# Numerators of batches 1 to 3 as float32 products on quarters of the array

## The chip, the core and the metric

The kernel runs on one core of a Trainium2 chip. A core has five engines that run side by side: TensorE (PE in the profile, with PEld for its loads of the stationary operand), VectorE (DVE), ScalarE (ACT), GpSimd (POOL), and SyncE (SP), which issues the DMAs. The metric is the time of one execution on the device, in microseconds (us); lower is better.

## The reference

Four batches go through a linear attention and then a gated layer whose gate mixes over the sequence. Cut to what matters:

```python
# batch 4, heads 4, seq 1088, head_dim 32, r = 8: 64 features per head
phi(x) = outer(S1 @ x, S2 @ x)                    # 64 products per position
kv = sum over seq of phi(k) * v                   # 64 x 32 per head
z = sum over seq of phi(k)
x = (phi(q) @ kv) / (phi(q) @ z + 1e-6)           # numerator / denominator
h = relu(x @ w_in); u, v = halves of h            # 512 + 512 columns
v_n = (v - mean(v)) / sqrt(var(v) + 1e-6)
out = (u * (w_spatial @ v_n + b_spatial)) @ w_out
```

The product with `w_spatial` (1088 x 1088 by 1088 x 512 for each batch) is most of the work.

## The kernel before

**Two kinds of product.** Large products are made of three float32r products each (`mm3`, lines 461 to 463): an operand x is split into a rounded high half (float32r) and a low half (x minus the high half), and high by high, high by low and low by high are added up in PSUM. A float32 product does without the split. The kernel has float32 products where operands are small: the projections of keys (L624), the sums over keys (L674) and the projections of queries (L797).

**Stages.** Batch 0's attention comes first and is written differently. The attention of batch b+1 (`attention`) is mixed into the large product of batch b (`main`, lines 1042 to 1053); batch 3's large product is another scheme (`main_fast`, lines 1314 to 1327). In `attention` a batch's 1088 positions are taken as three groups g of 384, 384 and 320 columns (`TW`). For each group and each pair of heads pr:

- DMAs bring the two factors `fa` and `fb` of the query features into slots of tag `pl`, and GpSimd multiplies them in place (L817). This is f, 128 features (two heads of 64) by n columns.
- ScalarE rounds f to its high half `fh` (L544) and GpSimd makes the low half `fl` (L474). Both lie in slots of tag `r`.
- TensorE takes `mm3` of f with `kvh`/`kvl`, the two halves of a 128 x 128 matrix for each pair with numerators and denominators of both heads and zeros between the heads. The result `nd` fills one PSUM bank of tag `sd` (there are two such banks).
- ScalarE takes the denominators out (L876, with 1e-6 added) and the numerators (L877), 64 partitions at a time, so that they lie alike.

Then VectorE takes the reciprocal (L878) and multiplies (L879), ScalarE and VectorE split the result into `xh` and `xl` (L544, L471), and three `mm3` with `w_in` make the h product (`hidden_v`, out to `sd` banks, ScalarE's L898).

The 128 x 128 matrices come from `kv`, the sums over keys: one ScalarE copy out of PSUM (L716), four VectorE products with a mask (L857), one cast and one subtraction (L544, L471).

**Order.** `ORDER` is a table of operation numbers, found beforehand by a planner. It sets the order of the instructions on every engine, the DMA queue's too; an engine does its instructions in this order and waits where an operand isn't ready. A prime mark behind a number chooses the other engine for an operation that has one.

Of the kernel before, what the change touches and what calls it, by code (L numbers as in the profile page):

```python
# [9 lines left out]
F32 = mybir.dt.float32  # L10
# [32 lines left out]
BIAS = [(0, 8, 53), (8, 4, 83), (12, 4, 83)]  # L43

# [11 lines left out]
    "pl": 6, "c": 3, "r": 4, "abT": 2, "kt": 3, "v": 3, "ka": 2, "kp": 3, "kvh": 1, "kvl": 1,  # L56
# [1515 lines left out]
```

## Time and profile before

| | |
|---|---|
| Time, median of 3 runs | 318.69 us (318.4 to 319.26) |
| Profiled execution | 318.51 us, of which the span shown is 316.7 us |
| PE busy | 311.3 us, 2717 products |
| DVE busy | 237.7 us |
| ACT busy | 171.8 us |
| POOL busy | 48.4 us |

The span runs from the first to the last instruction of the program; some 1.8 us of the execution lie around it. "Busy" is the time in which at least one instruction of the engine was under way. A PE product's record reaches from its start to the modelled end of its results, and the next one starts earlier than that: what a product takes from the engine is the distance from its start to the next start.

### The profile page before, as it was taken

How to read it: one execution, taken by the hardware profiler on the slowest of the kernel's cores; microseconds unless marked ns; L12 is line 12 of the kernel's file. 1: busy time of each engine (PE TensorE's matmuls, PEld its weight loads, DVE VectorE, ACT ScalarE, POOL GpSimd, SP SyncE). 2: the span in 40 equal slices, each digit the busy share in tenths (PEclk: the TensorE clock that was granted, in tenths of full speed). 3: DMA queues.
4: the chain of work that ended last, by engine and by line, in shares of the span. 5: the costliest groups of instructions: out<-in, count | busy, mean ns of one | idle time of the engine just before them, and what ended most of it. 6: DMA issues, size and time to landing. Idle time of an engine off the chain costs nothing.

```text
span 316.7 us, 7095 instructions
## 1 busy us (share of the span) xinstructions
PE 311.3 (98%) x2717; PEld 298.3 (94%) x2717; DVE 237.7 (75%) x551; ACT 171.8 (54%) x423; POOL 48.4 (15%) x63
## 2 busy tenths in 40 slices
PE   7999999999999999999999999999999999999996
PEld 6887999999999999999889999999999999999995
DVE  5999997365787956558896789879887987863445
ACT  2499956445774354465637557563254468442432
POOL 2000100764600001642003352100000000000000
PEclk9999999999999999999999999999999999999999
DMA  6942256646213036510113433422122333210001
GB/s 207 330 146 68 72 168 190 209 124 184 59 52 96 14 106 190 170 41 0 50 35 108 132 120 84 123 59 78 54 73 54 91 99 108 79 38 2 0 2 70
DMA packets 26019, 30.77 MB, mean 97 GB/s; under 512 B 3330, under 2 KB 25730, under 8 KB 25986
## 3 DMA queue, kind: packets, MB, share of 16 engines
q1 hardware_dynamic: 25986, 30.33, 32.1%
q8 instruction: 21, 0.34, 0.5%
q14 instruction: 12, 0.10, 0.1%
HBM read 27.25 MB, written 3.06 MB: 96 GB/s over the span
## 4 chain that ended last, share of the span: by engine, by line
PE 97%; DVE 1%; issue 0%; ACT 0%
PE sp L1042 16%; PE sp L1044 14%; PE sp L1051 14%; PE sd L461 4%; PE sd L462 4%; PE sd L463 4%; PE pu L461 3%; PE sd L1314 3%; PE sd L1316 3%; PE sd L1315 3%; PE pu L462 2%; PE pu L463 2%; PE po L461 2%; PE sp L1314 2%; PE sp L1316 2%; PE sp L1315 2%
## 5 line engine op out<-in xcount | busy, mean ns | idle before, releaser
L1042 PE MATMUL sp<-wT,vh 128*128 128x332 f32 (+1 forms) x306 | 98.8, 323 | 0.0
L1044 PE MATMUL sp<-wT,vl 128*128 128x332 f32 (+1 forms) x272 | 87.6, 322 | 0.0
L1051 PE MATMUL sp<-wT,vh 128*128 128x332 f32 (+1 forms) x272 | 85.9, 321 | 0.0
L1042 PEld LDWEIGHTS sp<-wT,vh 128*128 128x128 f32 x306 | 57.5, 188 | 1.8 <-issue 0.8
L1044 PEld LDWEIGHTS sp<-wT,vl 128*128 128x128 f32 x272 | 51.1, 188 | 0.6
L1051 PEld LDWEIGHTS sp<-wT,vh 128*128 128x128 f32 x272 | 51.0, 188 | 0.1
L900 DVE BATCH_NORM_STATS2 small<-vt 128x6 f32<-128x512 f32 x36 | 24.2, 683 | 7.1 <-ACT vt L898 7.1
L1078 DVE TENSOR_TENSOR u<-sp,u 128x332 f32<-128x332 f32 (+1 forms) x32 | 16.7, 523 | 17.0 <-PE sp L1053 9.1
L898 ACT ACTIVATE vt<-sd 128x512 f32<-128x512 f32 x36 | 21.5, 601 | 11.4 <-PE sd L463 10.6
L878 DVE RECIPROCAL area<-area 128x384 f32<-128x384 f32 (+1 forms) x9 | 21.7, 2415 | 7.5 <-ACT area L876 7.5
L817 POOL TENSOR_TENSOR area<-area 128x384 f32<-128x384 f32 (+1 forms) x18 | 17.3, 970 | 56.2 <-DVE vh L967 26.5
L544 ACT CAST g<-u 128x332 fp32r<-128x332 f32 (+1 forms) x32 | 15.5, 487 | 18.0 <-DVE u L1078 9.4
L474 POOL TENSOR_TENSOR area<-area,area 128x384 fp32r<-128x384 f32 (+1 forms) x18 | 18.0, 1006 | 19.8 <-ACT area L544 9.7
L1034 ACT ACTIVATE u<-pu 128x332 f32<-128x332 f32 (+1 forms) x32 | 14.9, 467 | 10.8 <-PE pu L463 9.5
L471 DVE TENSOR_TENSOR g<-u,g 128x332 fp32r<-128x332 f32 (+1 forms) x32 | 17.2, 536 | 2.5 <-ACT g L544 1.4
L596 ACT CAST wT<-area 128x332 fp32r<-128x332 f32 (+1 forms) x27 | 12.4, 495 | 9.4 <-DMA area<-in_wT 9.2
L631 DVE TENSOR_TENSOR area<-ka,sd 128x768 f32<-128x768 f32 x15 | 13.7, 947 | 4.3 <-ACT ka L629 4.2
L461 PE MATMUL pu<-x,wih 128*128 128x332 f32 (+3 forms) x52 | 16.6, 320 | 0.0
L462 PE MATMUL pu<-x,wih 128*128 128x332 f32 (+3 forms) x52 | 16.3, 314 | 0.0
L463 PE MATMUL pu<-x,wil 128*128 128x332 f32 (+3 forms) x52 | 16.3, 314 | 0.0
L920 DVE TENSOR_SCALAR vt<-vt,small 128x512 f32<-128x512 f32 x31 | 15.9, 537 | 0.0
L958 ACT CAST vh<-vt 128x384 fp32r<-128x384 f32 x24 | 12.1, 516 | 6.8 <-DVE vt L920 6.8
(239 smaller groups left out, 762.5 us busy)
## 6 DMA issues: line engine op xcount, KB each, us to landing
w<-in_wT SPq DMA_DIRECT2D x48, 138.0 KB
area<-in_wT SPq DMA_DIRECT2D x18, 166.0 KB
area<-in_vA SPq DMA_DIRECT2D x12, 198.0 KB
area<-in_kT SPq DMA_DIRECT2D x12, 192.0 KB
area<-abd SPq DMA_DIRECT2D x24, 96.0 KB
area<-abd SPq DMA_DIRECT2D x12, 192.0 KB
area<-in_wT SPq DMA_DIRECT2D x9, 212.0 KB
area<-in_qT SPq DMA_DIRECT2D x7, 192.0 KB
```

The lines of the kernel that those rows point to most:

```text
L461: nc.tensor.matmul(o, ah, bh, start=start, stop=False)
L462: nc.tensor.matmul(o, ah, bl, start=False, stop=False)
L463: nc.tensor.matmul(o, al, bh, start=False, stop=stop)
L471: return lambda: nc.vector.tensor_tensor(out=o(), in0=a(), in1=bb(), op=ALU.subtract)
L474: return lambda: nc.gpsimd.tensor_tensor(out=o(), in0=a(), in1=bb(), op=ALU.subtract)
L817: op("POOL", c_pool(n), lambda fa=fa, fb=fb: nc.gpsimd.tensor_tensor(out=fa[:, :n], in0=fa[:, :n], in1=fb[:, :n], op=ALU.mult), r=[fb], w= ...
L878: op("DVE", 135 + 6.3 * n, lambda x32=x32, n=n: nc.vector.reciprocal(out=x32[:, :n], in_=x32[:, :n]), w=[x32])
L898: op("ACT", c_act(512, True) + 16, lambda pv=pv, t=t: nc.scalar.activation(vt[:, t], pv.ap, AF.Relu), r=[pv], w=[(vt, toks(t))])
L900: op("DVE", 690, lambda stats=stats, t=t: nc.vector.bn_stats(out=stats.ap, in_=vt[:, t]), r=[(vt, toks(t))], w=[stats])
L1042: nc.tensor.matmul(sp[:, :cw], vh[:, kt], wTh[:, kt, cs], start=(kt == 0), stop=False)
L1044: nc.tensor.matmul(sp[:, :cw], vl[:, kt], wTh[:, kt, cs], start=False, stop=False)
L1051: nc.tensor.matmul(sp[:, :cw], vh[:, kt], wTl[:, kt, cs], start=False, stop=False)
```

## The change

1. The split of f, `fh`, `fl`, `kvh`, `kvl` and the mask products are gone. In their place a group has four float32 products of 64 x 64 by n columns, one on each quarter of the array: rows (features) of head a, columns of pair pr. Those of a = 0 write one `sd` bank, those of a = 1 the other, and the pair chooses the upper or lower 64 partitions.
2. `kd`, the 64 x 64 blocks, is written by two ScalarE copies out of PSUM in place of L716, L857 and the split.
3. Numerators and denominators now lie interleaved by 32 partitions, so they are taken out in six pieces (two of 128 partitions that write more than is wanted, and four of 32 that put it right) in place of four. Each piece has ScalarE and, as the other choice, VectorE.
4. The room of tag `r` goes to four more slots of tag `pl` (10 in place of 6) and to `kd`.
5. `ORDER` is new from the 449th entry on, sought with a charge for each change between float32 and float32r on TensorE.

```diff
-    "pl": 6, "c": 3, "r": 4, "abT": 2, "kt": 3, "v": 3, "ka": 2, "kp": 3, "kvh": 1, "kvl": 1,
+    "pl": 10, "c": 3, "abT": 2, "kt": 3, "v": 3, "ka": 2, "kp": 3, "kd": 2,
...
-419 441 564 399 384 442 443 444 560 561 415 385 400 445 565 421 422 423 424 425 426 427 428 429 267 554 258 579 259 268 562 420 260 530 531 532 580 111 282 269 563 546 279 541
+419 441 564 399 384 442 443 444 560 561 415 385 400 445 565 421 422 423 424 425 426 427 428 429 267 554 258 259 268 562 420 260 530 531 532 111 282 269 563 546 279 541 433 466
...
-        kvs = tl("ka", f"kvs{b}", [P, 68])
-        op("ACT", c_act(68, True), lambda: nc.scalar.copy(out=kvs.ap, in_=kv[:, :68]), r=[kv], w=[kvs])
-        return kvs
+        kd = tl("kd", f"kd{b}", [P, 2, 2, D])
+        def half(den):
+            o = kv[:, :68].rearrange("p (r c) -> p r c", r=2)
+            return nc.scalar.copy(out=kd[:, :, den], in_=o[:, :, D:D + 1].broadcast_to([P, 2, D]) if den else o[:, :, :D])
+
+        for den in range(2):
+            op("ACT", c_act(64, True), lambda den=den: half(den), r=[kv], w=[(kd, den)])
+        return kd
...
+            fs = [query_fs[b, g, pr] for pr in range(2)]
+            nds = [bank("sd", f"nd{b}{g}{a}") for a in range(2)]
+
+            def sums(fs=fs, nds=nds, n=n):
+                for pr in range(2):
+                    for a in range(2):
+                        rows = slice(64 * a, 64 * a + 64)
+                        nc.tensor.matmul(nds[a][64 * pr:64 * pr + 64, :n], kd[rows, pr].rearrange("p q d -> p (q d)"), fs[pr][rows, :n], start=True, stop=True)
+
+            op("PE", n * 4 / 2.35 + 220, f4=True, fn=sums, r=[kd, *fs], w=nds)
+
+            def take(out, a, den, q, at, key, n=n, nds=nds):
+                rows, src = slice(32 * q, 32 * q + at), nds[a]
+                i = slice(32 * (q ^ 1), 32 * (q ^ 1) + 32) if at == 32 else rows
+
+                def act():
+                    if den:
+                        return nc.scalar.activation(out[rows, :n], src[i, :n], AF.Copy, bias=ATT_EPS)
+                    return nc.scalar.copy(out=out[rows, :n], in_=src[i, :n])
+
+                def dve():
+                    if den:
+                        return nc.vector.tensor_scalar_add(out[rows, :n], src[i, :n], ATT_EPS)
+                    return nc.vector.tensor_copy(out=out[rows, :n], in_=src[i, :n])
+
+                op("ACT", c_act(n, True), act, r=[src], w=[(out, key)], alts=[("DVE", c_dve(n), dve)])
+
+            take(xn, 0, 0, 0, P, None)
+            take(x32, 1, 1, 0, P, None)
             for pr in range(2):
-                f = query_fs[b, g, pr]
-                fh, fl = tl("r", f"fh{b}{g}{pr}", [P, 384], F32R), tl("r", f"fl{b}{g}{pr}", [P, 384], F32R)
-                split(lambda fh=fh, n=n: fh[:, :n], lambda fl=fl, n=n: fl[:, :n], lambda f=f, n=n: f[:, :n], n, [f], [fh], [fl], pool=True)
-                nd = bank("sd", f"nd{b}{g}{pr}")
-                op("PE", c_mm(n, 3), cls=(n, 3), fn=lambda nd=nd, fh=fh, fl=fl, pr=pr, n=n: mm3(nd[:, :n], kvh[:, pr], kvl[:, pr], fh[:, :n], fl[:, :n]), r=[kvh, kvl, fh, fl], w=[nd])
...
+                take(xn, 1, 0, 2 * pr + 1, 32, pr)
+                take(x32, 0, 1, 2 * pr, 32, pr)
```

On TensorE, batch 1's first group stands at the same place of the order. Before (`pu0` is a gate product, `sd` the numerators' banks, `sp1` the large product's sum, `area2` the room of `fh`, `fl`, `kvh` and `kvl`):

```order
L463 MATMUL pu0_187<-x_77,wil0_72 128x332
L461 MATMUL sd0_94<-area2_80 128x384
L462 MATMUL sd0_94<-area2_80 128x384
L463 MATMUL sd0_94<-area2_80 128x384
L461 MATMUL sd1_119<-area2_80 128x384
L462 MATMUL sd1_119<-area2_80 128x384
L463 MATMUL sd1_119<-area2_80 128x384
L1042 MATMUL sp1_276<-wT_74,vh_67 128x332
```

And in the changed kernel (line numbers are two to sixteen higher there; `area2` now holds `kd` and slots of `pl`):

```order
L465 MATMUL pu0_187<-x_77,wil0_72 128x332
L869 MATMUL sd0_94<-area2_80 64x384
L869 MATMUL sd1_119<-area2_80 64x384
L869 MATMUL sd0_94<-area2_80 64x384
L869 MATMUL sd1_119<-area2_80 64x384
L1058 MATMUL sp1_276<-wT_74,vh_67 128x332
```

Six float32r products became four float32 products in a row, which alternate between the two banks, with float32r products before and behind them.

On ScalarE, what stands between batch 1's sums over keys and the first h product before (`ka0<-sd1` takes the sums out, `area2<-area0` rounds the matrices, `wT<-area1` rounds a piece of `w_spatial`, `area0<-po2` takes a result of batch 0 out, `x<-area1` rounds the attention's result, `vt<-sd0` is the h product's):

```order
L716 COPY ka0_63<-sd1_119 128x68
L544 CAST area2_80<-area0_78 128x256
L596 CAST wT_74<-area1_79 128x332
L1015 COPY area0_78<-po2_262 128x424
L876 ACTIVATE area1_79<-sd0_94 64x384
L876 ACTIVATE area1_79<-sd1_119 64x384
L1034 ACTIVATE u1_243<-pu0_187 128x332
L877 COPY area1_79<-sd0_94 64x384
L544 CAST area2_80<-area1_79 128x384
L877 COPY area1_79<-sd1_119 64x384
L544 CAST g_698<-u0_239 128x332
L544 CAST x_77<-area1_79 128x384
```

And in the changed kernel:

```order
L720 COPY area2_80<-sd1_119 128x2x32
L598 CAST wT_74<-area1_79 128x332
L1031 COPY area0_78<-po2_262 128x424
L879 ACTIVATE area1_79<-sd1_119 128x384
L879 ACTIVATE area1_79<-sd0_94 32x384 x2
L1050 ACTIVATE u1_243<-pu0_187 128x332
L880 COPY area1_79<-sd0_94 128x384
L880 COPY area1_79<-sd1_119 32x384 x2
L546 CAST g_698<-u0_239 128x332
L546 CAST x_77<-area1_79 128x384
```

Three pieces of denominators stand ahead of the reciprocal where two stood, and three pieces of numerators behind it where two stood; the round of f is gone.

On ScalarE in batch 2, from the first group's h products to the second group's numerators before (`vt<-sd` takes an h product out, the bank's number is behind `sd`):

```order
L898 ACTIVATE vt_82<-sd1_119 128x512
L898 ACTIVATE vt_82<-sd0_94 128x512
L544 CAST g_698<-u1_243 128x424
L898 ACTIVATE vt_82<-sd1_119 128x512
L544 CAST area2_80<-area1_79 128x320
L876 ACTIVATE area1_79<-sd0_94 64x384
L1034 ACTIVATE u2_250<-pu0_187 128x332
L876 ACTIVATE area1_79<-sd1_119 64x384
```

And in the changed kernel:

```order
L914 ACTIVATE vt_82<-sd1_119 128x512
L914 ACTIVATE vt_82<-sd0_94 128x512
L546 CAST g_698<-u2_250 128x424
L879 ACTIVATE area1_79<-sd0_94 128x384
L880 COPY area1_79<-sd1_119 128x384
L1050 ACTIVATE u0_239<-pu0_187 128x332
L880 COPY area1_79<-sd0_94 32x384 x2
L914 ACTIVATE vt_82<-sd0_94 128x512
```

The third h product of the first group moved behind the second group's numerators, and it takes bank `sd0` when the last of these pieces is out. On TensorE twelve products of the large one and three of the output, all of 424 columns, stand between those numerators and that h product.

## Rows read from the trace of the kernel before

**Rows 1.** The page: busy time of PE, and its granted clock in 40 slices.

```profile
PE 311.3 (98%) x2717; PEld 298.3 (94%) x2717; DVE 237.7 (75%) x551; ACT 171.8 (54%) x423; POOL 48.4 (15%) x63
...
PEclk9999999999999999999999999999999999999999
```

**Rows 2.** The page: chain that ended last, by engine.

```profile
PE 97%; DVE 1%; issue 0%; ACT 0%
```

**Rows 3.** Busy time in two stretches: us, each engine (instructions), clock, DMA share.

```profile
30.00:70.88 40.88, 40.88 (x435) 39.68 (x435) 30.04 (x68) 25.76 (x60) 12.14 (x15) 1.00 0.52 152
213.00:300.00 87.00, 87.00 (x623) 86.66 (x622) 65.99 (x164) 39.36 (x107) 0.00 (x0) 1.00 0.23 63
```

**Rows 4.** Timeline of PE, numerators of 384 columns, then 320: start, length.

```profile
70.88 0.34 PE L461 MATMUL sd<-area 128*128 128x384 f32 x1
...
71.77 0.34 PE L463 MATMUL sd<-area 128*128 128x384 f32 x1
71.94 0.32 PE L1042 MATMUL sp<-wT,vh 128*128 128x332 f32 x1
...
200.89 0.31 PE L461 MATMUL sd<-area 128*128 128x320 f32 x1
...
201.61 0.31 PE L463 MATMUL sd<-area 128*128 128x320 f32 x1
201.76 0.32 PE L1042 MATMUL sp<-wT,vh 128*128 128x332 f32 x1
```

**Rows 5.** Groups of PE by line and form: count, busy us, mean ns.

```profile
L461 PE MATMUL sd<-area 128*128 128x384 f32 x12 | 4.0, 337 | 0.0
...
L461 PE MATMUL sd<-area 128*128 128x320 f32 x6 | 1.9, 316 | 0.0
```

**Rows 6.** Timeline of PE, two late starts among the numerators.

```profile
92.27 0.36 PE L461 MATMUL sd<-area 128*128 128x320 f32 x1
92.47 0.31 PE L462 MATMUL sd<-area 128*128 128x320 f32 x1
...
130.31 0.44 PE L462 MATMUL sd<-area 128*128 128x384 f32 x1
130.59 0.34 PE L463 MATMUL sd<-area 128*128 128x384 f32 x1
```

**Rows 7.** Timeline of PE, from float32r to float32 (L674) and back.

```profile
66.69 0.31 PE L1044 MATMUL sp<-wT,vl 128*128 128x332 f32 x1
66.83 0.31 PE L1051 MATMUL sp<-wT,vh 128*128 128x332 f32 x1
67.07 1.73 PE L674 MATMUL sd<-area 128*32 128x33 f32 x144
68.73 0.47 PE L461 MATMUL po<-x,woh 128*128 128x424 f32 x1
69.04 0.35 PE L462 MATMUL po<-x,woh 128*128 128x424 f32 x1
69.23 0.35 PE L463 MATMUL po<-x,wol 128*128 128x424 f32 x1
```

**Rows 8.** Timeline of PE, float32 products of 192 columns on halves and on quarters of the columns.

```profile
22.16 0.87 PE L797 MATMUL po<-u,sk 128*64 128x192 f32 x8
22.96 0.50 PE L461 MATMUL sd<-wi,x 128*128 128x512 f32 x1
...
106.35 0.51 PE L797 MATMUL sd<-area,sk 128*32 128x192 f32 x8
106.79 0.46 PE L1042 MATMUL sp<-wT,vh 128*128 128x424 f32 x1
```

**Rows 9.** Timelines of ACT, DVE and PE: batch 1's first group, denominators to h product.

```profile
72.84 1.00 ACT L876 ACTIVATE area<-sd 64x384 f32<-64x384 f32 x2
...
73.87 2.55 DVE L878 RECIPROCAL area<-area 128x384 f32<-128x384 f32 x1 [2.84 <-ACT area L876]
...
77.67 0.56 DVE L471 TENSOR_TENSOR x<-area,x 128x384 fp32r<-128x384 f32 x1 [0.58 <-ACT x L544]
...
78.42 0.40 PE L461 MATMUL sd<-wi,x 128*128 128x512 f32 x1
```

More of the change, by code (lines that the diff above doesn't have):

```diff
@@ L43 @@
 BIAS = [(0, 8, 53), (8, 4, 83), (12, 4, 83)]
+PL_MIDDLE, EXTRA = 6, 2048
 TW = (384, 384, 320)
@@ L98 @@
 270 555 437 356 230 534 409 261 410 411 412 369 370 535 556 271 397 398 438 439 440 277 262 402 403 413 25 26 414 278 266 275 559 558 533 529 542 434 435 263 371 386 272 536
[40 rows of a table removed]
[10 rows of a table added]
+955 832 956 966 968 967 758 971 969 785 786 787 788 703 945 972' 970' 973 740 974 789 780 790 756 946 781 975 976 791 998 1000' 754 1002 1004 999 1003 1001 1005 1006 1007 755
[6 rows of a table added]
+1311 1054 1314 1139 1315 1318 1055 1319 1196 1044 879 1331 1409 1035 1316 1419 1317 1140 878 1333 1335 1332 1420 1337' 880 1410 1336 1338 1411 1421 1334 1339 1144 1340 1045
+1046 1047 1048 1049 1050 1423 1290 1293 1291 1341 1292 1296 1059 1060 1061 1062 1063 1064 882 1069 881 863 1065 1051 1052 1053 1193 1433 1342 1343 1094 1095 1096 1097 1098 1422
+1432 1434 1312 1313 1363 1365' 1090 1435 1066 1143 1367 1369 1424 1364 1436 1320 1370 1089 1427 864 1437 1428 1425 1426 1366 883 1070 1368 1371 1372 1091 884 1071 1072 1073
[19 rows of a table added]
 """
@@ L378, in tile_kernel @@
     early = {"kt": 384, "v": 396, "kp": 768}
-    middle = {"c": 384, "abT": 192, "pl": 424}
-    extra = {"r": 384, "kvh": 256, "kvl": 256}
-    parts = (early, middle, extra)
-    sizes = [sum(n * Order.bufs(t) for t, n in part.items()) for part in parts]
-    areas = [const.tile([P, n], F32R if j == 2 else F32, name=f"area{j}", tag=f"area{j}", bufs=1) for j, n in enumerate(sizes)]
-    spans, again = [], {2: areas[2]}
+    middle = {"c": (384, 0, 3), "abT": (192, 0, 2), "pl": (424, 0, PL_MIDDLE)}
+    extra = {"pl": (424, PL_MIDDLE, Order.bufs("pl")), "kd": (128, 0, 2)}
+    parts = ({t: (n, 0, Order.bufs(t)) for t, n in early.items()}, middle, extra)
+    sizes = [max(sum(n * (e - a) for n, a, e in part.values()), EXTRA * (j == 2)) for j, part in enumerate(parts)]
+    areas = [const.tile([P, n], F32, name=f"area{j}", tag=f"area{j}", bufs=1) for j, n in enumerate(sizes)]
+    spans, again = [], {}
     for j, (area, part) in enumerate(zip(areas, parts)):
         end = 0
-        for tag, n in part.items():
-            m = Order.bufs(tag)
-            homes[tag] = area[:, end:end + m * n].rearrange("p (n c) -> p n c", n=m)
-            homes |= {(tag, i): homes[tag][:, i] for i in range(m)}
+        for tag, (n, a, e) in part.items():
+            m = e - a
+            home = area[:, end:end + m * n].rearrange("p (n c) -> p n c", n=m)
+            if m == Order.bufs(tag):
+                homes[tag] = home
+            homes |= {(tag, a + i): home[:, i] for i in range(m)}
             spans += [(j, end + i * n, end + i * n + n, tag) for i in range(m)]
@@ L849, in attention @@
         k.part = "k", f"k{b}"
-        kv = keys(b, qts)
-        kd = tl("kp", f"kd{b}", [P, 4, 2, D])
-        for pr in range(2):
-            for den in range(2):
-                def part(pr=pr, den=den):
-                    v = kv[:, 34 * pr:34 * pr + D + 1].unsqueeze(1)
-                    src = (v[:, :, D:] if den else v[:, :, :D]).broadcast_to([P, 2, D])
-                    return nc.vector.tensor_tensor(out=kd[:, 1 + pr if den else 3 * pr], in0=src, in1=mask[:, 2:4].unsqueeze(2).broadcast_to([P, 2, D]), op=ALU.mult)
-                op("DVE", 215, part, r=[kv, mask], w=[(kd, (pr, den))], sh=True)
-        kvh, kvl = tl("kvh", f"kvh{b}", [P, 2, P], F32R), tl("kvl", f"kvl{b}", [P, 2, P], F32R)
-        split(
-            lambda: kvh.ap.rearrange("p r c -> p (r c)"), lambda: kvl.ap.rearrange("p r c -> p (r c)"), lambda: kd.ap.rearrange("p q a d -> p (q a d)"),
-            256, [kd], [kvh], [kvl],
-        )
+        kd = keys(b, qts)
         for g in range(3):
@@ L868, in attention @@
             x32, xn = tl("c", f"x32{b}{g}", [P, 384]), tl("c", f"xn{b}{g}", [P, 384])
-            for pr in range(2):
-                f = query_fs[b, g, pr]
-                fh, fl = tl("r", f"fh{b}{g}{pr}", [P, 384], F32R), tl("r", f"fl{b}{g}{pr}", [P, 384], F32R)
-                split(lambda fh=fh, n=n: fh[:, :n], lambda fl=fl, n=n: fl[:, :n], lambda f=f, n=n: f[:, :n], n, [f], [fh], [fl], pool=True)
-                nd = bank("sd", f"nd{b}{g}{pr}")
-                op("PE", c_mm(n, 3), cls=(n, 3), fn=lambda nd=nd, fh=fh, fl=fl, pr=pr, n=n: mm3(nd[:, :n], kvh[:, pr], kvl[:, pr], fh[:, :n], fl[:, :n]), r=[kvh, kvl, fh, fl], w=[nd])
-                rows, den = slice(64 * pr, 64 * pr + 64), slice(64 - 64 * pr, 128 - 64 * pr)
-                op("ACT", c_act(n, True), lambda nd=nd, x32=x32, rows=rows, den=den, n=n: nc.scalar.activation(x32[rows, :n], nd[den, :n], AF.Copy, bias=ATT_EPS), r=[nd], w=[(x32, pr)])
-                op("ACT", c_act(n, True), lambda nd=nd, xn=xn, rows=rows, n=n: nc.scalar.copy(out=xn[rows, :n], in_=nd[rows, :n]), r=[nd], w=[(xn, pr)])
+            fs = [query_fs[b, g, pr] for pr in range(2)]
@@ L1082, in gate @@
             else:
-                tag = "r" if last(d) else "g"
-                gh, gl = tl(tag, f"gh{b}{d}{c}", [P, cw], F32R), tl(tag, f"gl{b}{d}{c}", [P, cw], F32R)
+                gh, gl = tl("g", f"gh{b}{d}{c}", [P, cw], F32R), tl("g", f"gl{b}{d}{c}", [P, cw], F32R)
                 parts = [(lambda: gh.ap, gh), (lambda: gl.ap, gl)]
@@ L1141, in weights_fast @@
     def weights_fast():
-        whole = {tag: Whole(k, tag, f"s_{tag}", [P, n], F32 if part is not extra else F32R) for part in parts for tag, n in part.items()}
+        whole = {tag: Whole(k, tag, f"s_{tag}", [P, n]) for part in parts for tag, (n, _, _) in part.items()}
         whole["g"] = Whole(k, "g", "s_g", [P, G_PITCH], F32R)
```

73 rows, old and new, of the table ORDER are left out of this document.

## The prediction

> **What bounds the kernel now.** I read the page first: PE is busy for 311.3 of 316.7 us, at the full granted clock in all 40 slices [rows 1]. The chain that ended last is 97% PE and 1% DVE [rows 2], so the end is set by TensorE. Busy shares are averages, so I then took stretches: from 30 us to the end of batch 1's sums, and from 213 to 300 us, PE is busy for every microsecond, while DVE has 30.04 of 40.88 and 65.99 of 87.00 [rows 3]. The reader is to see that there is hardly any idle time on PE to win. What can shorten this kernel is less work on PE, and what can lengthen it is more work on PE or a wait put in front of it. Work taken from ScalarE, VectorE and GpSimd counts only through such a wait.
>
> A busy PE is not yet a PE at its peak, since records overlap. So I go by distances between starts: a float32r product of 384 columns takes (71.94 - 70.88) / 6 = 0.177 us, one of 320 columns (201.76 - 200.89) / 6 = 0.145 us [rows 4]. Products of 332 columns follow each other at 0.14 to 0.15 us and those of 424 at 0.19 us [rows 7].
>
> **What is removed from PE.** The two groups of rows are those of the first line of `mm3`, with 12 and 6 products [rows 5]; the other two lines have as many, so 36 products of 384 columns and 18 of 320 go: 36 x 0.177 + 18 x 0.145 = 6.37 + 2.61 = 8.98 us. Two of them carried a wait inside the numerators: a step of 0.20 in place of 0.145 us at 92.27 and one of 0.28 in place of 0.177 us at 130.31 [rows 6]. Both sit in the first two products of a pair's three, where what can be late is a half of f; that split no longer exists. With these 0.16 us the removal is worth 9.14 us. What is late next at those places is f itself, GpSimd's product, which lay ahead of the split and so was there earlier; I count nothing for it.
>
> **What is added to PE.** Nine visits to float32, one per group; in the new order each stands alone, with float32r products on both sides. The trace has no product of 64 x 64, so I build a visit from three pieces.
>
> Going in: the last float32r product ahead of L674 takes 67.07 - 66.83 = 0.24 us where its neighbour takes 0.14, so 0.09 to 0.10 us. Coming back: the first float32r product takes 69.04 - 68.73 = 0.31 us where the next of its kind takes 0.19, so 0.12 us [rows 7].
>
> The inside: four products of 192 columns on halves of the columns, two at a time, take 22.96 - 22.16 = 0.80 us; four of the same length on quarters of the columns, all at a time, take 106.79 - 106.35 = 0.44 us [rows 8]. So the second round of 192 columns costs 0.36 us, part of which is that the first of these stretches pays its weight loads and the second follows other float32 products; two equal rounds and one fixed part fit with 0.33 us a round and 0.14 us fixed. The same rows show that tiles on different columns run side by side, even where they read different moving data (here two halves of the queries). Four quarters that run side by side are one round of 384 or 320 columns: 0.66 + 0.14 = 0.80 us or 0.55 + 0.14 = 0.69 us. With the change of kind on both sides, 0.21 us, a visit is 1.01 or 0.90 us, and nine are 6 x 1.01 + 3 x 0.90 = 8.76 us.
>
> From below, the fixed part could be hidden, as most of it is in the second stretch (0.44 - 0.33 = 0.11, so at least a part stays): nine times 0.14 less is 7.50 us. From above, nothing shows that the two row halves of the array run side by side; if they don't, a visit has two rounds, and nine cost 6 x 0.66 + 3 x 0.55 = 5.61 us more, 14.37 us. I take 8.76: the rows nearest to it are those of tiles that do run together, and the two halves of the rows here read different partitions and write different banks.
>
> The Trainium skill has a rule for the inside, in "TensorE: Matmul & The Clock Gate", section "Measured speedup vs the span model": tiles packed in the array span one product plus some 4 ns for each further tile. By that rule the fixed part falls away and the sum would be 0.01 us per visit above the lower bound just given; the trace speaks against it in part, since 0.11 us stay on top of a round in the better of the two stretches.
>
> **What is added and removed elsewhere.** ScalarE loses 18 rounds of f, three copies and three rounds of the matrices, and gets two to three more pieces a group less those that VectorE takes (in the order nine of 54 pieces go to VectorE). GpSimd loses half of its work in these stages. VectorE loses twelve products with the mask and three subtractions. None of these engines is full, so I cost them at nothing as work; the cover is PE's large product. What counts is the chain from numerators to h product. In batch 1's first group two denominators end at 73.84, the reciprocal runs from 73.87, the low half ends at 77.67 + 0.56 = 78.23, and PE starts the h product at 78.42 [rows 9]: 0.19 us to spare. In five of the nine groups that margin is 0.5 us or less (by the same reading 0.09 to 0.48), in the other four over 1.5. A third piece of denominators in front of the reciprocal is worth 1.00 / 2 = 0.5 us [rows 9]. Against that stand a group that begins earlier relative to its sums (the mask products and the split of the matrices are gone) and ScalarE's round of f, which stood among the pieces. I take nothing for it, and keep up to 0.5 us in five groups as a bound.
>
> More slots of `pl` let SP issue loads of `w_spatial` and of the factors earlier. Nothing on PE waits for them from 30 us on [rows 3], so this is worth nothing; the first 50 us of the order are as before.
>
> **Sum.** 318.51 - 9.14 + 8.76 = 318.13 us by the profiled execution, which lies 0.18 us below the median of the three runs; against that the forecast is 318.3 us, 0.1% faster, and so nothing that a measurement of this kernel tells from no change (about 0.3%, 0.96 us). I predict 318.3 us, with 317.5 to 319.2 for this case alone.
>
> **The rivals.**
>
> *The row halves take turns.* Then the quarters are two rounds: 318.3 + 5.6 = 323.9 us, slower. For it: no row shows two row halves at once. Against it: halves and quarters of the columns run at once [rows 8]. The change then doesn't do what it says. 0.10.
>
> *The fixed part is hidden.* A visit is 0.14 us cheaper, nine are 1.26 us: 317.0 us, faster. For it: only a part shows in the second stretch of [rows 8]. Against it: that stretch follows float32 products, while a visit comes out of float32r, and the weights of the quarters are as wide as those of the first stretch. The rule named above would come out here. 0.14.
>
> *Pieces come out late.* Each group now holds both `sd` banks until six pieces are out, and the reciprocal stands behind three denominators. In batch 2's second group ScalarE has, behind the numerators, four pieces and a gate piece to do before the third h product of the first group gets `sd0`: 4 x 0.5 + 0.45 = 2.45 us, while PE has fifteen products of 424 columns, 15 x 0.19 = 2.85 us. This decides for PE from the point where ScalarE starts more than 0.4 us late. Five groups with a margin below 0.5 us that lose what the third piece costs beyond it, (0.5 - 0.23) each, are 1.35 us: 319.7 us, slower; if they lose all of it, 320.8. "TensorEngine Tiling (Array Packing)", section "PSUM Bottleneck", of the Trainium skill speaks for this rival: tiling speeds up TensorE but not the emptying of PSUM, which can become the limit. Here a group's pieces go from four to six at the same 0.5 us each. 0.14, of which 0.10 slower and 0.04 within.
>
> *The order alone.* From 30 us on PE's steps show only a handful of waits, and those outside the numerators come to little; an order that fills them all would bring about 0.6 us, an estimate from the same reading of starts: 317.7 us, on the edge. 0.08, half of it faster.
>
> **How the numbers follow.** The forecast has 0.54: 0.11 of it faster by over 0.3% (visits a tenth of a microsecond cheaper, or waits gone), 0.42 within, 0.01 slower. With the rivals: faster 0.11 + 0.14 + 0.04 = 0.29, within 0.42 + 0.04 + 0.04 = 0.50, slower 0.01 + 0.10 + 0.10 = 0.21. The range goes down to 317.0, where the fixed part is hidden, and up to 320.3, where pieces are late in five groups with most of their price; outside lie the row halves taking turns (0.10) and about 0.08 on the two sides.
>
> **What the profile of the changed kernel would show.** L869, the numerators: eight records of a visit in two bunches, all within about 0.4 us, and some 0.80 us (384 columns) from the first to the next float32r start; 1.4 us or more means that row halves take turns, 0.66 that the fixed part is hidden. The product ahead of a visit should take 0.09 us more than its kind, the one behind it 0.12. The steps of 0.20 and 0.28 us in the numerators should be gone. L463 out to `sd` should start without idle time ahead of it; if it starts over 0.1 us behind L473's end with PE waiting, or the step before it is longer than its kind, the pieces are late. The prediction is wrong if the visits don't cost what three pieces of other shapes say, or if the new order makes PE wait in places that the change doesn't touch.

## The result, and the profile after

The changed kernel takes 321.17 us (median of 4 runs, 320.95 to 321.98) against 318.91 us before: a ratio of 1.0072, with a 95% interval of 1.0058 to 1.0087. It is 2.3 us slower, where 318.3 us were forecast; that is outside the stated range of 317.5 to 319.2 us, and outside the 317.0 to 320.3 us by which the chances go. The profiled execution took 321.98 us, its span 319.9 us.

The page first, the lines that answer to [rows 1] and [rows 2]: busy time of each engine, PE's granted clock, and the chain that ended last.

```profile
PE 314.4 (98%) x2735; PEld 292.4 (91%) x2735; DVE 238.8 (75%) x545; ACT 168.5 (53%) x414; POOL 31.3 (10%) x45
...
PEclk9999999999999999999999999999999999999999
...
PE 56%; DVE 1%; issue 0%; ACT 0%
```

PE is as full as before and its granted clock is at the full level in all 40 slices, yet PE is busy for 3.1 us longer. The chain's shares, 97% PE before, now add up to 57%: followed back from the end, it stops at a reciprocal of VectorE at 133.27 us, after 58% of the span. That is the third place below. For the other waits I went through the distances between PE's starts, as in the prediction, and took every one that is longer than its kind.

Timeline of PE, the first visit (L869, batch 1's first group); the columns are start, length, engine, line, operation, operands and count.

```profile
71.42 0.31 PE L465 MATMUL pu<-x,wil 128*128 128x332 f32 x1
71.67 0.88 PE L869 MATMUL sd<-area 64*64 64x384 f32 x8
72.47 0.42 PE L1058 MATMUL sp<-wT,vh 128*128 128x332 f32 x1
72.73 0.31 PE L1060 MATMUL sp<-wT,vl 128*128 128x332 f32 x1
```

This is what was forecast. The step in is 0.25 in place of 0.15 us, the inside 0.80, the step behind it 0.26 in place of 0.15. The eight records start in two bunches of four, 0.37 us apart: the quarters run side by side. Eight of the nine visits take 0.806 us (384 columns) or 0.699 us (320); the forecast had 0.80 and 0.69.

The same view for the second visit, batch 1's second group:

```profile
81.36 0.40 PE L465 MATMUL sd<-wi,x 128*128 128x512 f32 x1
81.69 1.29 PE L869 MATMUL sd<-area 64*64 64x384 f32 x3
82.45 0.54 PE L869 MATMUL sd<-area,area 64*64 64x384 f32 x2
...
83.24 0.42 PE L1058 MATMUL sp<-wT,vh 128*128 128x332 f32 x1
```

And the timelines of ACT and PEld at that place, with the idle time before an instruction and what ended it in brackets:

```profile
81.79 0.60 ACT L914 ACTIVATE vt<-sd 128x512 f32<-128x512 f32 x1 [0.56 <-PE sd L465]
...
82.44 0.13 PEld L869 LDWEIGHTS sd<-area 64*64 64x64 f32 x1 [0.57 <-ACT vt L914]
```

The first quarter starts at once, into the bank that is free. The second needs the bank of the h product that ended just ahead (L465 at 81.36), ACT's relu holds it until 82.39, and the other two quarters stand behind the second on PE. The visit takes 83.24 - 81.69 = 1.55 us, 0.75 more than the others.

The third place is batch 2's first group, whose visit stands at 129.08. Timelines of DVE, of GpSimd and of ACT there, then of PE at its h product:

```profile
130.10 0.56 DVE L884 TENSOR_SCALAR area<-sd 128x384 f32<-128x384 f32 x1 [5.36 <-PE sd L869]
131.74 0.56 DVE L884 TENSOR_SCALAR area<-sd 32x384 f32<-32x384 f32 x1 [1.09 <-ACT area L879]
132.34 0.60 DVE L1094 TENSOR_TENSOR u<-sp,u 128x424 f32<-128x424 f32 x1
132.85 0.41 DVE L976 TENSOR_TENSOR vl<-vt,vh 128x256 fp32r<-128x256 f32 x1
133.19 2.55 DVE L894 RECIPROCAL area<-area 128x384 f32<-128x384 f32 x1
...
136.96 1.06 DVE L473 TENSOR_TENSOR x<-area,x 128x384 fp32r<-128x384 f32 x1 [0.17 <-ACT x L546]
...
136.60 2.29 POOL L824 TENSOR_TENSOR area<-area,area 128x384 f32<-128x384 f32 x2 [9.79 <-DVE area L895]
...
131.23 0.48 ACT L879 ACTIVATE area<-sd 32x384 f32<-32x384 f32 x1
...
136.66 0.35 PE L1067 MATMUL sp<-wT,vh 128*128 128x424 f32 x1
136.98 0.50 PE L463 MATMUL sd<-wi,x 128*128 128x512 f32 x1
137.32 0.40 PE L464 MATMUL sd<-wi,x 128*128 128x512 f32 x1
138.07 0.50 PE L465 MATMUL sd<-wi,x 128*128 128x512 f32 x1 [0.36 <-DVE x L473]
138.41 0.39 PE L463 MATMUL sd<-wi,x 128*128 128x512 f32 x1
```

DVE's second piece starts when ACT's piece out of the same bank is done, 1.09 us after DVE was free; then a gate (L1094) and a low half of v (L976, "the features' low half" below) stand ahead of the reciprocal. It starts 3.30 us behind the end of the visit at 129.89. In the kernel before it was 0.72 us there, from 130.77 to this reciprocal; DVE's timeline of before:

```profile
131.48 2.55 DVE L878 RECIPROCAL area<-area 128x384 f32<-128x384 f32 x1 [0.80 <-ACT area L876]
...
135.26 0.56 DVE L471 TENSOR_TENSOR x<-area,x 128x384 fp32r<-128x384 f32 x1 [0.58 <-ACT x L544]
```

The low half of x, which the h product's third round needs, ends at 138.02. PE's steps there are 0.32, 0.34, 0.75 and 0.34 us where 0.19 and, three times, 0.235 would do: 0.86 us. In the kernel before, the low half ended at 135.82, 0.10 us ahead of the first round and 0.57 us ahead of the third; this margin has turned into a wait. By these times some half a microsecond of it lies in the low half itself, which takes 1.06 us in place of 0.56: a product of GpSimd (L824) runs beside it. In the twelve traces of this case the 148 low halves of x with no GpSimd instruction beside them take 0.48 to 0.60 us, and the eight beside this product 1.06 to 1.25.

The fourth is behind batch 3's second group: a DVE piece waits 0.94 us for ACT's piece of the same bank, and the reciprocal starts at 195.74, 2.34 us behind the visit's end, where it was 1.22 us before. Here the h product's third round is late by under 0.03 us; but DVE has the gate (L1094) behind the low half, and the next product of the large one needs the `sp` bank that this gate frees. It loses 0.30 us, and the step behind it 0.11 us. DVE's timeline, then PEld's:

```profile
195.15 0.56 DVE L884 TENSOR_SCALAR area<-sd 32x384 f32<-32x384 f32 x1 [0.94 <-ACT area L880]
195.74 2.55 DVE L894 RECIPROCAL area<-area 128x384 f32<-128x384 f32 x1
...
201.14 0.19 PEld L1058 LDWEIGHTS sp<-wT,vh 128*128 128x128 f32 x1 [0.35 <-DVE u L1094]
```

These three waits are 0.75 + 0.86 + 0.41 = 2.02 us. The other excess after 60 us is without a releaser in the trace: 0.49 us between two products of the large one at 170.4 ("issue"), some 0.5 us in the sums over the keys of batches 1 and 2, and 0.17 us in small steps. Of such steps the kernel before has 0.16 us in the numerators [rows 6] and about 0.2 us elsewhere before its last products. So 2.02 + 1.17 - 0.34 us of waits and 0.3 us of work less make some 2.5 us in this execution, an estimate from the starts, against 2.3 us between the medians.

### The profile page after: what moved, and what is told of

It reads as the page before. It is cut to its first block, busy times and chain, and to the rows that moved or that the text cites. A ratio compares the mean times of both kernels' runs of the same rounds, so it can differ in the third digit from the quotient of the medians.

```text
span 319.9 us, 7092 instructions
## 1 busy us (share of the span) xinstructions
PE 314.4 (98%) x2735; PEld 292.4 (91%) x2735; DVE 238.8 (75%) x545; ACT 168.5 (53%) x414; POOL 31.3 (10%) x45
## 4 chain that ended last, share of the span: by engine, by line
PE 56%; DVE 1%; issue 0%; ACT 0%
PE sp L1058 9%; PE sp L1060 7%; PE sp L1067 7%; PE sd L1329 3%; PE sd L1331 3%; PE sd L1330 3%; PE sp L1329 2%; PE sp L1331 2%; PE sp L1330 2%; PE pu L463 2%; PE pu L464 2%; PE pu L465 2%; PE sd L465 1%; PE po L463 1%; PE sd L464 1%; PE sd L463 1%
## 5 line engine op out<-in xcount | busy, mean ns | idle before, releaser
L473 DVE TENSOR_TENSOR g<-u,g 128x332 fp32r<-128x332 f32 (+1 forms) x32 | 18.0, 564 | 11.1 <-ACT g L546 5.8
L1094 DVE TENSOR_TENSOR u<-sp,u 128x332 f32<-128x332 f32 (+1 forms) x32 | 16.6, 520 | 10.8 <-PE sp L1069 7.5
L465 PE MATMUL pu<-x,wil 128*128 128x332 f32 (+3 forms) x52 | 16.4, 314 | 0.0
L465 PE MATMUL sd<-wi,x 128*128 128x512 f32 x36 | 14.4, 400 | 0.4 <-DVE x L473 0.4
L463 PE MATMUL sd<-wi,x 128*128 128x512 f32 x36 | 14.7, 408 | 0.0
L464 PE MATMUL sd<-wi,x 128*128 128x512 f32 x36 | 14.3, 396 | 0.0
L546 ACT CAST x<-area 128x384 fp32r<-128x384 f32 (+2 forms) x13 | 6.5, 511 | 14.6 <-DVE area L895 11.3
```

Source lines behind the costliest of these rows:

```text
L463: nc.tensor.matmul(o, ah, bh, start=start, stop=False)
L464: nc.tensor.matmul(o, ah, bl, start=False, stop=False)
L465: nc.tensor.matmul(o, al, bh, start=False, stop=stop)
L473: return lambda: nc.vector.tensor_tensor(out=o(), in0=a(), in1=bb(), op=ALU.subtract)
L546: op("ACT", c_act(n), lambda: nc.scalar.copy(out=hi(), in_=x()), r=r, w=wh)
L1094: op("DVE", c_dve(cw), lambda: nc.vector.tensor_tensor(out=u.ap, in0=sp[:, :cw], in1=u.ap, op=ALU.mult), r=[sp], w=[u], lead=LEAD[1])
```

## The experiments

Two theories were set against each other at first. Q: the quarters cost the time, wherever they stand, because a visit needs two `sd` banks at once and a chain of six pieces follows. O: the new places in `ORDER` cost it. The short diffs below show pieces of `ORDER`; 601 is the visit of batch 1's second group, 461 and 463 are the step of the large product and the output product behind which it is moved. ("Gate product" in the expectations is such a step of the large product, `sp`.) In the kernels with an edited table the same lines of code have numbers five lower than in the changed kernel (L864 for L869).

**The changed kernel again** (no edit).

> The changed kernel a second time, as the yardstick for the others and to learn which of its waits come back. Both theories say 321.2 us (320.9 to 321.6). The waits that are tied to the program must return at the same places and sizes: 0.75 us inside the visit of batch 1's group 2 (first quarter starts, the next half only when ACT's relu has let go of the other sd bank), about 0.85 us in the h product of batch 2's first group (it waits for the low half), about 0.44 us behind batch 3's group 2. The waits that have no releaser in the trace, 0.32 us in batch 2's sums over the keys and 0.49 us between two gate products near 170 us, should be elsewhere or gone if they are chance, and return if they belong to the program.

Measured: 321.58 us, 1.0076 (1.0059 to 1.0094). The three waits with a releaser come back within 0.01 us of their sizes (0.75, 0.87, 0.41). The one near 170 us comes back smaller (0.33 for 0.49), and the sums over batch 2's keys take 2.38 us, against 2.44 and, in the kernel before, 2.12. Since they return at the same places, these belong to the program or its timing and not to one execution, though nothing names their cause.

**The quarters under the order of before.** The numbers of `ORDER` are those of before, with each visit in the place of the second pair's numerators (some pieces a few places later, where an operand wasn't there yet). All 54 pieces are ScalarE's here, where the new order gives nine to VectorE.

> The quarters under the order of before: every visit stands where the second pair's numerators stood, its six pieces where the copies stood. Theory Q, the quarters themselves cost the time (two sd banks held at once, a chain of six pieces, whatever the places): 320.5 to 321.5 us, with waits of 0.4 to 0.8 us inside the visits that stand right behind an h product, and h products that wait for their low half. Theory O, the new places cost the time: 318.3 to 318.9 us, near the forecast of 318.3 us, with under 1 us of waits in all. In both the matmul work stays 0.3 us below that of before.

Measured: 322.27 us, 1.0091 (1.0067 to 1.0116). O as the sole cause falls: there are waits in the old places too, and those for a bank hang on ACT's relu, not on which engine takes the pieces. Four visits are now stretched by the second bank: that at 81.49 by 0.75 us, and three by 0.29 to 0.30 us. PE's timeline of one of these, batch 3's second group:

```profile
192.65 0.31 PE L460 MATMUL po<-g,wol 128*128 128x332 f32 x1
192.90 1.17 PE L864 MATMUL sd<-area,area 64*64 64x384 f32 x8
194.00 0.46 PE L1053 MATMUL sp<-wT,vh 128*128 128x424 f32 x1
```

Ahead of it ACT's relu runs from 192.55 to 193.15; the first quarter starts at 192.90, the second at 193.20. The visit takes 1.10 us where 0.81 is the rule. Other waits are at h products (0.26 us and two steps of 0.11 near 137), at a product of the large one behind the visit at 146.83 (0.36) and near 186 and 198 (0.44 and 0.31). So the order of before loses more in the banks (1.63 against 0.75 us), and both lose in the chains behind the visits; how much of the latter here comes from having all pieces on ScalarE no run shows.

**One visit later.**

```diff
-552 548 581 601 461 483 463 484 603 607
+552 548 581 461 483 463 601 484 603 607
```

> The changed kernel with one entry of ORDER moved: the visit of batch 1's group 2 stands behind the next gate product and the next output product instead of ahead of them (about 0.9 us later). Both sd banks are free by then. If the wait inside that visit is the two banks and what is late next is not the chain behind it, the visit takes 0.81 us instead of 1.56 us and the time is 320.4 us (0.75 us less than the changed kernel). If the wait only moves on to that group's h product, the time stays at 321.2 us.

Measured: 321.68 us, 1.0075 (1.0057 to 1.0092); nothing is won. PE's timeline shows both halves of it, and ACT's the way between them:

```profile
82.05 0.54 PE L864 MATMUL sd<-area 64*64 64x384 f32 x2
...
82.85 0.42 PE L1053 MATMUL sp<-wT,vh 128*128 128x332 f32 x1
...
85.77 0.31 PE L460 MATMUL po<-g,wol 128*128 128x332 f32 x1
86.64 0.42 PE L458 MATMUL pu<-x,wih 128*128 128x332 f32 x1 [0.57 <-ACT u L1045]
...
83.12 1.50 ACT L874 ACTIVATE area<-sd 128x384 f32<-128x384 f32 x3 [0.93 <-PE sd L864]
84.66 1.46 ACT L875 COPY area<-sd 128x384 f32<-128x384 f32 x3
86.14 0.45 ACT L1045 ACTIVATE u<-pu 128x332 f32<-128x332 f32 x1
```

The visit takes 0.80 us, as it should. But ACT now starts the six pieces later, and L1045, which empties the `pu` bank, stands behind them in ACT's order. 0.73 us come back at the next product into `pu`. The wait has moved on to another place than the group's h product, which was the second case of the expectation.

**Three places mended.** Beside the edit above, in batch 2's first group (738 the gate, 777 the features' low half, 940' DVE's second piece) and in batch 3's second group (1337' is DVE's piece, 1337 the same one on ACT):

```diff
-935 939 938 940' 738 742 777 941 937 942
+935 939 938 738 777 940' 742 941 937 942
...
-878 1333 1335 1332 1420 1337' 880 1410 1336
+878 1333 1335 1337 1332 1420 880 1410 1336
```

> The changed kernel with three places mended and the quarters untouched: the visit of batch 1's group 2 behind the next two products; in batch 2's group 1 the gate and the features' low half of DVE ahead of its second piece, which stood idle there, so that the reciprocal starts 0.88 us earlier; in batch 3's group 2 DVE's piece given to ACT, so that the reciprocal starts 0.6 us earlier. Theory O, the places cost the time: 0.75 + 0.86 + 0.44 = 2.05 us less than the changed kernel, 319.1 us (318.7 to 319.6). Theory Q, the quarters cost it anywhere: the waits come back at other places and the time stays above 320.5 us.

Measured: 320.56 us, 1.0034 (1.0019 to 1.005). The waits of 0.86 and 0.41 us are gone, the 0.73 us at `pu` are back as in the last run. The median stands just inside Q's range (above 320.5 us); by the ratio it would be 320.0 us beside 318.91, between the two theories. So this run decides little; the next one goes on from its one large wait.

**A fourth entry**: 465 empties the `pu` bank; 602, 604 and 606 are the numerator pieces.

```diff
-486 487 474 602 604 606 465 583 462 587
+486 487 474 465 602 604 606 583 462 587
```

> The three mended places and one entry more: batch 1's group 2 had its wait come back as 0.73 us at a later hidden-layer product, whose pu bank ACT empties behind the visit's six pieces; here ACT empties that bank behind the three denominator pieces, ahead of the three numerator pieces, which have the reciprocal's 2.55 us to be done in. If that queue is all that gave the 0.75 us back, the time falls by 0.73 us to 319.8 us (319.3 to 320.2); if the visit's lateness is handed on again, it stays at 320.5 us.

Measured: 319.25 us, 1.0001 (0.9984 to 1.0018). With four entries of `ORDER` the loss is gone, within 0.2%. From 1.0034 to 1.0001 are some 1.0 us, a little more than the 0.73 us expected; the steps at this place account for 0.56 us of it, and the intervals leave room for the rest. ACT's timeline: L1045, which empties `pu`, stands between the pieces of the denominators and of the numerators, and PE's wait at `pu` falls from 0.73 to 0.07 us (with two steps of 0.1 us behind it).

```profile
83.95 1.50 ACT L874 ACTIVATE area<-sd 128x384 f32<-128x384 f32 x3 [0.93 <-PE sd L864]
85.48 0.45 ACT L1045 ACTIVATE u<-pu 128x332 f32<-128x332 f32 x1
85.82 1.46 ACT L875 COPY area<-sd 128x384 f32<-128x384 f32 x3
```

**Without the small pieces.** The changed kernel in its own order, without

```diff
-            for pr in range(2):
-                take(xn, 1, 0, 2 * pr + 1, 32, pr)
-                take(x32, 0, 1, 2 * pr, 32, pr)
```

> The changed kernel, its order kept, without the four 32-row pieces of each group (36 in all, so half of the heads' rows are taken from the wrong bank): the quarters and their two banks stay, the chain behind a visit is as short as a copy of 128 rows for each bank. Theory C, the long chain of pieces makes the h products late: the waits of 0.86 us in batch 2's first h product and 0.44 us behind batch 3's group 2 go, the 0.75 us inside the visit of batch 1's group 2 stays, and the time is 320.0 us. Theory B, the two banks are the whole cost: these waits stay and the time stays at 321.2 us or above.

Measured: 319.93 us, 1.0027 (1.0013 to 1.0042), where theory C said 320.0 us. The waits at batch 2's h product and behind batch 3's are gone: the reciprocals start 1.53 and 0.74 us behind their visits, in place of 3.30 and 2.34. The visit at 81.35 still takes 1.56 us: it waits for a relu, not for a piece. The page shows what left: 15 us of ACT, and 2 us of DVE.

```profile
PE 312.8 (98%) x2735; PEld 292.4 (92%) x2735; DVE 236.6 (74%) x540; ACT 153.3 (48%) x383; POOL 31.4 (10%) x45
```

**Later visits in the order of before.** The visits 601, 633, 966, 998 and 1331 one to three products later, and 465 as above.

> The quarters under the order of before, with the five visits that lost 0.29 to 0.75 us inside (1.98 us in all) moved behind one to three more products, and ACT's emptying of pu ahead of the numerator pieces in batch 1's group 2. If the two banks are a matter of where the visits stand, the visits take 0.81 and 0.70 us and the time falls from 322.3 us towards 320.3 us. If a later visit only makes its chain late, waits of the same sum stand at the h products or behind ACT, and the time stays near 322 us.

The 1.98 us in that text hold 0.36 us too many: at 146.83 all eight records start on time, and what is late is the product of the large one behind them. Four visits lost 1.63 us. Measured: 323.35 us, 1.0126 (1.0106 to 1.0145). All nine visits take 0.81 or 0.70 us, and the kernel is slower than with the stretched ones. Timeline of ACT, DVE and PE behind batch 2's second visit, which now ends at 142.14:

```profile
142.41 1.50 ACT L874 ACTIVATE area<-sd 128x384 f32<-128x384 f32 x3 [1.07 <-PE sd L864]
...
144.43 1.47 ACT L875 COPY area<-sd 128x384 f32<-128x384 f32 x3
...
146.24 0.52 ACT L1045 ACTIVATE u<-pu 128x424 f32<-128x424 f32 x1
...
146.79 0.60 DVE L1089 TENSOR_TENSOR u<-sp,u 128x424 f32<-128x424 f32 x1 [0.29 <-ACT u L1045]
...
147.45 0.42 PE L1053 MATMUL sp<-wT,vh 128*128 128x332 f32 x1 [1.25 <-DVE u L1089]
```

Six pieces hold ACT; L1045, which empties `pu` behind them, is late, so is the gate that reads its result, and PE waits 1.41 us for the `sp` bank that the gate frees. Taking the wait for a bank away by waiting elsewhere was no gain here.

**Batch 2's first group alone**: the edit of 738, 777 and 940' by itself.

> The changed kernel with only the edit in batch 2's first group: DVE's gate and low half of the features stand in the gap in which DVE waits for ACT's piece, ahead of its own second piece, so that the reciprocal starts 0.88 us earlier. If the 0.86 us of waits at that group's h products is the lateness of the chain and nothing takes its place, the time falls by 0.86 us to 320.3 us (ratio to before near 1.0045); if the wait is another's, the time stays at 321.2 us.

Measured: 320.01 us, 1.0033 (1.002 to 1.0047), 0.4% less than the changed kernel's 1.0076 in its second measurement; the 1.0045 expected lies inside the interval. The chain that ended last is 97% PE again. DVE fills the gap, and PE's h product starts without a wait, though the low half of x takes 1.07 us beside GpSimd here too: the reciprocal, 2.45 us behind the visit, leaves it the time.

```profile
129.39 0.59 DVE L1089 TENSOR_TENSOR u<-sp,u 128x424 f32<-128x424 f32 x1
129.90 0.42 DVE L971 TENSOR_TENSOR vl<-vt,vh 128x256 fp32r<-128x256 f32 x1
130.56 0.56 DVE L879 TENSOR_SCALAR area<-sd 32x384 f32<-32x384 f32 x1 [0.25 <-ACT area L874]
131.15 2.55 DVE L889 RECIPROCAL area<-area 128x384 f32<-128x384 f32 x1
...
135.66 0.40 PE L458 MATMUL sd<-wi,x 128*128 128x512 f32 x1
...
136.13 0.42 PE L460 MATMUL sd<-wi,x 128*128 128x512 f32 x1
```

The run with three places mended, which has this edit too, stands at 1.0034. Its other two edits thus show nothing in the time beside this one, though one of them takes a wait of 0.41 us out of the trace; the intervals, 0.15% to each side, hide that much.

**A fifth entry**: 482 empties the next `pu` bank, 592 is a square root.

```diff
-462 587 592 478 481 608 482 609 610 488
+462 587 478 481 608 482 592 609 610 488
```

> The kernel with four mended places and a fifth: in batch 1's group 2 ACT empties the next pu bank ahead of a square root that nothing waits for soon. The product that waits there lost 0.28 us in all; if that is given back the time is 0.1% below that of before (ratio 0.9985 to 0.9995, about 319.0 us where before has 319.3 us). Beating before by more than 0.3% is not expected by any theory: 0.3 us of matmul work less is all that the quarters bring here.

Measured: 319.41 us, 1.0015 (1.0003 to 1.0027). The gain that was expected is missing: the waits of 0.07 and 0.11 us at the product into `pu` now stand at the h product behind it, at 89.29. The kernel before isn't beaten.

**Before again**, for its profile.

> The kernel before a second time, for its profile alone: whether its few waits come back (0.7 us between 30 us and the end), and how far the start moves from run to run (the first h product at 18.0 us in the profile of before, at 18.5 to 19.0 us in those of the changed kernel). No theory expects another time than 318.9 us.

Measured: 319.01 us, span 317.2 us. The first h product stands at 18.28 us (18.02 in the first profile; 18.46 and 19.02 in those of the changed kernel), so the start moves by some tenths of a microsecond from run to run, in both kernels. Three of the small waits come back, 0.52 us at 70.4 to 71.4 are new, and the sums over batch 3's keys take 2.45 us in place of 2.20. A stretched sum is thus nothing that only the changed kernel has.

## Why the prediction was wrong

**Right: the work on PE.** Nine visits were forecast at 6 x 0.80 + 3 x 0.69 = 6.87 us inside and 1.89 us for the change of kind. Without the one stretched by a bank they measure 6 x 0.806 + 3 x 0.699 = 6.93 us and about 9 x (0.09 + 0.11) = 1.8 us. The removal of 8.98 us follows from the rows, and the two late starts of [rows 6] are gone. So the row halves don't take turns, and the fixed part isn't hidden. The split into 0.33 us a round and 0.14 us fixed does not follow from [rows 8], whose two stretches alone give 0.36 and 0.08 us; by either split a visit of 384 columns is 0.80 us. By the rule in "TensorE: Matmul & The Clock Gate", section "Measured speedup vs the span model", of the Trainium skill, a visit of 384 columns would come to some 0.67 us, an estimate with the round of 0.66 us from the prediction; the trace says 0.806, and the measurement decides.

**Wrong: "I take nothing for it".** That is the step that failed, in the part on what is added and removed elsewhere. It set the longer chain against a group's earlier begin and kept up to 0.5 us in five groups as a bound, outside the sum. In place of nothing the trace has 0.86 + 0.41 us at one h product and behind another, and leaving out the 32-row pieces takes both away and 0.45% of the time (1.0072 to 1.0027). The size was wrong as well: a third piece was priced at 0.5 us, while the way from the visit's end to the reciprocal grew by 2.58 and 1.12 us in these two groups (0.72 to 3.30, 1.22 to 2.34). Three things make the price. Six pieces of 0.5 us hold ACT for some 3 us, and PE depends on ACT for two other things, the relu that frees `sd` and L1045, which frees `pu`. At these two places a piece on DVE waits for ACT's piece out of the same bank (1.09 and 0.94 us), so giving it to DVE did not shorten the chain. And the low half of x in batch 2's first group fell beside a product of GpSimd and took 0.5 us more; mending the order of the pieces alone made room for that, so it is no cause by itself, and whether the wait would have been smaller without it was not run. The prediction read its margins, 0.09 to 0.48 us, up to the first round of the h product. The low half is needed in the third, 0.47 us later, so the margins that were lost are larger than it says.

**Wrong: both banks at once.** Holding both `sd` banks stood in the rival of the late pieces, but for another place (ScalarE's queue in batch 2's second group). No term of the sum stands for it. The wait came at batch 1's second group, where an h product ends just ahead of the visit: 0.75 us in the changed kernel's order, 1.63 us at four visits in the order of before. Before the change a group's numerators of the first pair needed one bank.

The rival *pieces come out late* had the mechanism, with 319.7 to 320.8 us, and was given 0.14; the time was above even that: not five groups lost but two, 1.27 us together, and the bank's 0.75 us and the excess without a releaser came on top. Its sentence from "TensorEngine Tiling (Array Packing)", section "PSUM Bottleneck", of the Trainium skill, that emptying PSUM can become the limit, is borne out by the run without the small pieces, though as the length of a chain and not as a full engine: ACT is busy for 53% of the span. The rival *order alone* hoped that a new order would fill waits; this one opened some. That the loss is no fixed price of the quarters, the edited tables show: 1.0001 with four entries, 1.0015 with five. Nor does the work won show: 0.3 us is below what these runs tell from nothing. Before's own numerators in the new order were not run.

**Open:** the step of 0.13 to 0.49 us near 170 us in all kernels in the new order and in none in the order of before. No releaser stands at it, and none of the edits was aimed at it. The sums over batch 2's keys go the same way: 2.11 to 2.13 us in the four traces in the order of before, two of them with the quarters, and 2.30 to 2.44 us in seven of the eight in the new order. So some 0.6 to 0.8 us of the excess in the two profiles of the changed kernel goes with the new order, with no cause shown.

## What to carry to other kernels

An operand layout that saves products may need more banks at once and more pieces to take out: price the emptying engine's queue, and ask whose bank, gate or relu stands behind those pieces, before counting it as free because the engine is half idle. A wait removed by moving an instruction can go to the next one in the same queue: here the visit moved alone won nothing, and when the instruction that empties `pu` was moved ahead of three pieces as well, the time fell by another 0.3% (1.0034 to 1.0001). And where the saving is 0.1% of the time, two margins of some tenths of a microsecond decide the sign.

## What was not expected of the hardware

Executions of one kernel differ in how fast the same products follow each other, with the granted clock at 1.00 in each. Between 32.5 and 43 us the starts of products of 424 columns are 0.197 us apart in one profile of a kernel and 0.187 in the other, and the records of one line last 361 and 348 ns; the groups of PE by form, the changed kernel in its two runs:

```profile
L1060 PE MATMUL sp<-wT,vl 128*128 128x424 f32 x15 | 5.4, 361 | 0.0
```

```profile
L1060 PE MATMUL sp<-wT,vl 128*128 128x424 f32 x16 | 5.6, 348 | 0.0
```

The kernel before has the same two, 361 ns in its first profile and 348 ns in its second. It makes some 0.5 us by the end of that stretch, as much as one of the waits above, and does not go with the change: single profiles of this kernel are compared step by step, not by their spans.
